# Attention with a learned bias, then a max-of-three layer: fewer identity products, other PSUM banks and another pace in the first steps

## The chip, the cores and the metric

The kernel runs on one NeuronCore of one Trainium2 chip. The metric is device time in microseconds (us): the median of three runs.

## What is computed

The first stage is attention for 4 batches, 8 heads, 576 positions and 64 features, with a bias that a small two-layer network makes of the distance of two positions. The second stage multiplies its output by three matrices, takes the largest of the three products and multiplies by a fourth.

```python
scores = scale * np.matmul(q, k.transpose(0, 1, 3, 2))
rel = (pos[:, None] - pos[None, :]).astype(np.float32)
x = (np.log1p(np.abs(rel)) / psi_i)[..., None]
bias = np.maximum(x @ w1 + b1, 0.0) @ w2
scores = scores + bias.transpose(2, 0, 1)[None, :, :, :]
attn = np.exp(scores - np.max(scores, axis=-1, keepdims=True))
attn = attn / (np.sum(attn, axis=-1, keepdims=True) + 1e-09)
x = (attn @ v)            # then laid out as 2304 tokens by 512
h = np.maximum(np.maximum(x @ w1, x @ w2), x @ w3)
return h @ w_out
```

## The kernel before

**Bias stage.** 36 groups of 16 rows: VectorE (DVE) and ScalarE (ACT) make the hidden layer, TensorE (PE) multiplies by `w2s` into `bp` tiles of two PSUM banks, DVE or ACT scale them into `bs`, and SyncE's queue (SP) writes them to DRAM as `bias_d`, from where the tiles `bias0` to `bias4` are read. Ahead of it stand four products `wps` of a tile of zeros.

**Attention stage.** Heads go in pairs; a unit is one pair of heads of one batch, and 16 units make 8 pairs of units. A pair of units has nine steps (`NS` = 9), so 72 steps are numbered n = 0 to 71, and a step's place in its pair is n % 9. Each step takes 128 query rows of two heads; one of the nine (`y == MIX`) takes the 64 rows left over of both units. What step n does, by function:

- `front(n)`: PE makes the scores `s` of both heads, two tiles of two PSUM banks each: 12 products, as the operands are split into a high part (`kh`, `qh`) and a low part (`kl`, `ql`). In the first `FILL` = 4 steps four products of the identity (L265), whose result is overwritten at once, stand ahead of them. In these four steps the score tiles rotate through four buffers, eight banks; afterwards through two buffers, four banks, and the other four banks hold `l`, `t` and `pv`.
- up to three items are taken from the list `pvq` (L422 on): an item is one block of the product of attention and values (`pv`), five items make a group, and `pv` is a single bank. The first item of a group first calls `split_x`, which writes the DVE copies (`xb`) of the group before into the program.
- `shift(n, h)`: DVE adds the bias to the scores and finds the minimum `nm` (L290), for each of the two heads; `expo(n, h)`: ACT makes the exponentials (L304).
- `norm(n-2)`: GpSimd (POOL) multiplies by the reciprocal of the sums (L318). `flip(n-4)`: PE transposes (tiles `tp`, `lp`), and ACT (L431, L432) and DVE (L434) copy the result into `et`. Where a group of transposes is complete (`ends`), the second exponential of the step stands behind these copies instead of ahead of them.
- `prep`: the split of a later unit's operands. ACT makes the high parts `kh`, `qh` (L242), POOL subtracts for the low parts `kl`, `ql` (L245).
- the stream `w0`: conversion of the weights of the second stage from 64-bit words, one instruction per step at most: one on ACT (L546) and four on DVE (L548, L550, L553, L556) for each half block, with sums and differences on POOL behind some of them. From step 7 on, each step but those with n % 9 == 8 carries one.

Each engine runs its instructions in the order in which these calls write them; nothing reorders them, so an instruction that waits holds up all behind it on its engine.

**Second stage.** Products `c` and `p` in three operand terms each, at L605 to L607 and L975 to L977, with DVE and ACT combining them.

## Time and profile before

| | |
|---|---|
| median of three runs | 554.94 us (554.85 to 555.05) |
| the profiled execution | 554.69 us |
| its span, first to last instruction | 552.9 us |
| busy in the span | PE 530.2, DVE 438.9, ACT 363.3, POOL 293.2 us |
| chain that ended last | PE 78%, DVE 10%, ACT 5%, issue 4% |

In a row of the windows view stand the stretch in us, its length, the busy time and in brackets the instructions of PE, PE's weight loads (PEld), DVE, ACT and POOL, PE's granted clock, the DMA engines' busy share and GB/s. In a timeline row stand start, length, engine, line, operation, output and inputs, shapes, count, and in square brackets the idle time before it and what ended it.

The span is cut here by the first `shift` of a pair of units: the bias stage ends at 51.76 us, the attention steps run to about 270 us, and the second stage starts at 282.4 us. A busy PE is modelled and says little by itself; the waits at its side, and which instruction stands ahead of the one that waited, say more.

### The profile page before, as it was taken

How to read it: one execution, taken by the hardware profiler on the slowest of the kernel's cores; microseconds unless marked ns; L12 is line 12 of the kernel's file. 1: busy time of each engine (PE TensorE's matmuls, PEld its weight loads, DVE VectorE, ACT ScalarE, POOL GpSimd, SP SyncE). 2: the span in 40 equal slices, each digit the busy share in tenths (PEclk: the TensorE clock that was granted, in tenths of full speed). 3: DMA queues.
4: the chain of work that ended last, by engine and by line, in shares of the span. 5: the costliest groups of instructions: out<-in, count | busy, mean ns of one | idle time of the engine just before them, and what ended most of it. 6: DMA issues, size and time to landing. Idle time of an engine off the chain costs nothing.

```text
span 552.9 us, 13740 instructions
## 1 busy us (share of the span) xinstructions
PE 530.2 (96%) x5231; PEld 438.3 (79%) x5231; DVE 438.9 (79%) x913; ACT 363.3 (66%) x814; POOL 293.2 (53%) x296
## 2 busy tenths in 40 slices
PE   8999888999999999999899999999999999999997
PEld 4456655666666666666589999999999999999997
DVE  7997668999988998887588888866887346798883
ACT  6997787898999989898766633434334335355552
POOL 0847475598988989766700328366386433600000
PEclk9999889999999999999999999999999999999999
DMA  5895971954594219311100424542256330467562
GB/s 142 226 342 163 337 241 23 304 196 144 146 340 125 58 25 297 90 24 40 43 2 2 152 77 135 190 153 78 76 207 212 116 127 16 140 205 210 178 186 76
DMA packets 74033, 80.75 MB, mean 146 GB/s; under 512 B 23216, under 2 KB 54576, under 8 KB 73968
## 3 DMA queue, kind: packets, MB, share of 16 engines
q1 hardware_dynamic: 73824, 79.58, 45.8%
q8 instruction: 41, 0.67, 0.5%
q10 hardware_dynamic: 144, 0.29, 0.2%
q14 instruction: 24, 0.20, 0.1%
HBM read 50.61 MB, written 28.99 MB: 144 GB/s over the span
## 4 chain that ended last, share of the span: by engine, by line
PE 78%; DVE 10%; ACT 5%; issue 4%; DMA 1%; POOL 1%; SPq 0%; DVEq 0%; ACTq 0%
PE pv L386 11%; PE p L607 10%; PE p L606 10%; PE p L605 10%; PE s L280 7%; PE tp L345 4%; PE p_o L977 4%; PE p_o L975 4%; PE p_o L976 4%; DVE hid L114 4%; PE bp L135 3%; ACT e L304 3%; DVE sn L290 2%; PE lp L345 2%; PE c L605 2%
## 5 line engine op out<-in xcount | busy, mean ns | idle before, releaser
L318 POOL TENSOR_SCALAR e<-e,rc 128x576 f32<-128x576 f32 x144 | 112.7, 801 | 36.0 <-DVE rc L314 28.6
L304 ACT ACTIVATE e<-sn,nm 128x576 f32<-128x576 f32 x144 | 111.5, 776 | 23.4 <-DVE nm L290 22.9
L290 DVE CUSTOM_DVE_ANT_0 sn<-s,bias 128x576 f32<-128x576 f32 x144 | 103.1, 753 | 19.6 <-PE s L280 11.6
L386 PE MATMUL pv<-et,vt 128*64 128x320 f32 (+1 forms) x496 | 75.2, 424 | 3.9 <-DVE xb L405 1.8
L497 POOL TENSOR_TENSOR wl<-wr,wh 128x256 fp32r<-128x256 f32 x25 | 23.6, 969 | 74.7 <-ACT wh L693 74.7
L434 DVE COPY et<-tp 128x512 f32<-128x512 f32 x72 | 49.0, 680 | 17.2 <-PE tp L345 13.9
L345 PE MATMUL tp<-ident,e 64*128 64x64 f32 x1152 | 55.3, 227 | 0.0
L280 PE MATMUL s<-kh,qh 64*128 64x288 f32 x256 | 51.2, 340 | 3.8 <-DVE nm L290 3.7
L386 PEld LDWEIGHTS pv<-et,vt 128*64 128x64 f32 x496 | 31.7, 138 | 29.1 <-issue 6.2
L245 POOL TENSOR_TENSOR kl<-kr,kh 128x576 fp32r<-128x576 f32 x16 | 39.4, 2462 | 24.1 <-ACT kh L242 23.0
L345 PEld LDWEIGHTS lp<-ident,e 64*128 64x128 f32 x144 | 19.8, 138 | 35.3 <-issue 23.4
L431 ACT COPY et<-tp 128x512 f32<-128x512 f32 x72 | 41.3, 574 | 8.6 <-PE lp L345 6.1
L345 PEld LDWEIGHTS tp<-ident,e 64*128 64x128 f32 x1152 | 45.4, 140 | 0.1
L135 PE MATMUL bp<-hid,w2s 128*32 128x79 f32 (+51 forms) x640 | 41.4, 401 | 3.3 <-DVE hid L114 2.1
L280 PE MATMUL s<-kl,qh 64*128 64x288 f32 x256 | 44.3, 299 | 0.0
L280 PE MATMUL s<-kh,ql 64*128 64x288 f32 x256 | 43.2, 296 | 0.9 <-POOL ql L245 0.9
L114 DVE TENSOR_SCALAR hid<-sm,bp 128x528 f32<-128x528 f32 (+17 forms) x108 | 41.4, 458 | 0.0
L345 PE MATMUL lp<-ident,e 64*128 64x64 f32 x144 | 35.3, 245 | 5.2 <-ACT et L432 2.7
L135 PEld LDWEIGHTS bp<-hid,w2s 128*32 128x32 f32 x640 | 20.6, 113 | 24.6 <-issue 15.5
L497 POOL TENSOR_TENSOR wl<-ws,wh 128x256 fp32r<-128x256 f32 x28 | 29.5, 1076 | 14.3 <-ACT wh L695 14.3
L280 PEld LDWEIGHTS s<-kh,qh 64*128 64x128 f32 x256 | 30.7, 191 | 7.1 <-DVE nm L290 6.2
L652 ACT COPY u<-p 128x384 f32<-128x384 f32 x24 | 11.5, 480 | 37.0 <-PE p L607 37.0
(229 smaller groups left out, 1622.0 us busy)
## 6 DMA issues: line engine op xcount, KB each, us to landing
bias_d<-bs SPq DMA_DIRECT2D x36, 295.5 KB, 5.5
bias<-bias_d SPq DMA_DIRECT2D x16, 576.0 KB, 6.0
w<-in_moe_w_dram SPq DMA_DIRECT2D x36, 256.0 KB, 3.3
h_d<-ht SPq DMA_DIRECT2D x18, 384.0 KB, 3.4
hin<-h_d SPq DMA_DIRECT2D x16, 384.0 KB, 4.6
qr<-in_qd_dram SPq DMA_DIRECT2D x16, 288.0 KB, 4.6
kr<-in_kd_dram SPq DMA_DIRECT2D x16, 288.0 KB, 5.3
vt<-in_v_dram SPq DMA_DIRECT2D x32, 128.0 KB, 2.9
```

The lines of the kernel that those rows point to most:

```text
L114: nc.vector.tensor_scalar(out=h[:, 0:n], in0=wl[:, 0:n], scalar1=k["bp"][:, m:m + 1], scalar2=0.0, op0=ALU.add, op1=ALU.max)
L135: nc.tensor.matmul(bp[32 * c:32 * c + 32, o:o + w], lhsT=w2s, rhs=src, start=True, stop=True)
L280: nc.tensor.matmul(ss[h][:, x, 0:HALF], lhsT=u[q][p, 128 * t:128 * t + 128], rhs=u[k][p, cols], start=(j == 0), stop=(j == 2))
L290: nc.vector.tensor_tensor_reduce(out=sn.rearrange("p (a b) -> p a b", a=2), in0=st["s"][h][:, :, 0:HALF], in1=bt.rearrange("p (a b) -> p a ...
L304: nc.scalar.activation(st["e"][:, S * h:S * h + S], sn, ACTF.Exp, scale=-1.0, bias=nm, accum_out=self.sm[:, x:x + 1])
L318: nc.gpsimd.tensor_scalar(out=e, in0=e, scalar1=self.rc[:, x:x + 1], scalar2=1.0, op0=ALU.mult, op1=ALU.mult)
L345: return nc.tensor.transpose(to, e2[p, k0:k0 + 128], ident[p, p])
L386: nc.tensor.matmul(pv[p], lhsT=w, rhs=x, start=(c == 0), stop=(c == NTQ))
L497: eng.tensor_tensor(out=out, in0=f(a), in1=f(b), op=op)
L605: nc.tensor.matmul(o, lhsT=hi[:, c], rhs=h[:, j], start=first and j == 0, stop=False, **on)
L606: nc.tensor.matmul(o, lhsT=hi[:, c], rhs=l[:, j], start=False, stop=False, **on)
L607: nc.tensor.matmul(o, lhsT=lo[:, c], rhs=h[:, j], start=False, stop=last and j == 1, **on)
```

## The change

- One of the four products of zeros ahead of the bias stage goes. As the bias products rotate through the same banks, each of them moves by one place.
- Identity products: none in step 0, two instead of four in steps 1, 2 and 3.
- The score tiles of the first four steps are two tags of two buffers, `s0` for even steps and `s1` for odd ones. As built, the two tiles of steps 0 and 2 lay in the banks from 0 and from 6 on, those of steps 1 and 3 in those from 4 and from 2 on; now steps 0 and 2 have 0 and 2, steps 1 and 3 have 4 and 6. From step 4 on the tiles lie at 0 and 2, before and now. The second tile of step 4 therefore waited for step 3, and now waits for step 2; the first transposes, at 4 to 6, now wait for step 3.
- In the first 18 steps at most three items of `pvq` are taken and none after the last of a group. Before, up to three were taken in the first 16 steps without regard to groups, and by the table after that.
- For the third unit (steps 6 and 7) DVE, not ACT, makes `kh` and `qh`.
- `ends` also holds for n % 9 == 7.
- The stream `w0` rests at n % 9 of 4, 5 and 8 instead of 8 alone.

On PE, the end of the bias stage (`bp31`) and step 0 (tiles `s0_0_0`, `s0_0_1`), before:

```order
L135 MATMUL bp31_881<-hid126_859,w2s_98 32x80
L135 MATMUL bp31_881<-hid127_857,w2s_98 32x80
L265 MATMUL s0_0_0_905<-ident_63 128x128 x4
L280 MATMUL s0_0_0_905<-kh0_244,qh0_320 128x288
L280 MATMUL s0_0_1_906<-kh0_244,qh0_320 128x288
L280 MATMUL s0_0_0_905<-kl0_245,qh0_320 128x288
```

and now:

```order
L134 MATMUL bp31_879<-hid126_857,w2s_96 32x80
L134 MATMUL bp31_879<-hid127_855,w2s_96 32x80
L279 MATMUL s0_0_0_903<-kh0_242,qh0_318 128x288
L279 MATMUL s0_0_1_904<-kh0_242,qh0_318 128x288
L279 MATMUL s0_0_0_903<-kl0_243,qh0_318 128x288
L279 MATMUL s0_0_1_904<-kl0_243,qh0_318 128x288
```

The four identity products between the last bias product and the first scores are gone.

On DVE, steps 10 and 11, where a group of products ends (`sn10`, `sn11` are the shifts, `wa3` the conversion), before:

```order
L314 RECIPROCAL rc8_1447<-sm8_1318 128x4
L434 COPY et1_1_1269<-tp0_6_1_1453 128x8x64
L548 TENSOR_SCALAR wa3_0_1411<-wa3_0_1411 128x512
L405 COPY xb11_0_1219<-pv0_1_1431 128x128
L405 COPY xb11_1_1223<-pv0_1_1431 128x128
L405 COPY xb11_1_1223<-pv0_1_1431 128x64
L290 ISA sn11_0_1506,nm11_0_1507<-s1_2_0_1482,bias2_76 128x576
L290 ISA nm11_0_1507 128x1
```

and now:

```order
L313 RECIPROCAL rc8_1435<-sm8_1306 128x4
L434 COPY et1_1_1255<-tp0_6_1_1441 128x8x64
L548 TENSOR_SCALAR wa3_0_1399<-wa3_0_1399 128x512
L289 ISA sn11_0_1488,nm11_0_1489<-s1_2_0_1470,bias2_76 128x576
L289 ISA nm11_0_1489 128x1
L289 ISA sn11_1_1493,nm11_1_1494<-s1_2_1_1471,bias2_76 128x576
L289 ISA nm11_1_1494 128x1
L405 COPY xb11_0_1207<-pv0_1_1419 128x128
L405 COPY xb11_1_1211<-pv0_1_1419 128x128
L405 COPY xb11_1_1211<-pv0_1_1419 128x64
```

The three copies of `pv0_1` stood between the conversion of step 10 and the shift of step 11, and now stand behind that shift. The same holds for the copies of `pv1_1` at steps 12 and 13.

On DVE, steps 22 and 23 (n % 9 of 4 and 5), before:

```order
L290 ISA nm22_1_2228 128x1
L556 SCALAR_TENSOR_TENSOR wr1_2231<-w642_0_1646,signm_64,wa2_0_1972 128x512
L314 RECIPROCAL rc20_2237<-sm20_2097 128x4
L434 COPY et4_0_2241<-tp2_0_1_2244 128x8x64
L290 ISA sn23_0_2294,nm23_0_2295<-s2_5_0_2276,bias0_74 128x576
L290 ISA nm23_0_2295 128x1
L290 ISA sn23_1_2299,nm23_1_2300<-s2_5_1_2277,bias0_74 128x576
L290 ISA nm23_1_2300 128x1
L405 COPY xb12_1_1222<-pv3_0_2214 128x192
L405 COPY xb12_2_1226<-pv3_0_2214 128x64
L434 COPY et4_0_2241<-tp2_1_1_2308 128x8x64
L548 TENSOR_SCALAR wa2_1_2236<-wa2_1_2236 128x512
```

and now:

```order
L289 ISA nm22_1_2211 128x1
L313 RECIPROCAL rc20_2214<-sm20_2074 128x4
L434 COPY et4_0_2218<-tp2_0_1_2221 128x8x64
L289 ISA sn23_0_2270,nm23_0_2271<-s2_5_0_2252,bias0_74 128x576
L289 ISA nm23_0_2271 128x1
L289 ISA sn23_1_2275,nm23_1_2276<-s2_5_1_2253,bias0_74 128x576
L289 ISA nm23_1_2276 128x1
L405 COPY xb12_1_1210<-pv3_0_2197 128x192
L405 COPY xb12_2_1214<-pv3_0_2197 128x64
L434 COPY et4_0_2218<-tp2_1_1_2284 128x8x64
```

The conversion instructions L556 and L548 no longer stand in these steps. The last conversion on DVE was in step 48, and now is in step 63.

```diff
--- before.py
+++ after.py
@@ -45,11 +45,10 @@
 
     const = ctx.enter_context(tc.tile_pool(name="const", bufs=1))
     psums = []
-    s_bufs = [4]
     dram = ctx.enter_context(tc.tile_pool(name="dram", bufs=1, space=DRAM))
 
-    def ps_s(name):
-        return psums[-1].tile([128, 2, 512], F32, tag="s", bufs=s_bufs[-1], name=name)
+    def ps_s(name, tag="s"):
+        return psums[-1].tile([128, 2, 512], F32, tag=tag, bufs=2, name=name)
 
     def bank(name):
         return psums[-1].tile([128, 512], F32, tag="p", bufs=8, name=name)
@@ -259,9 +258,9 @@
         def front(self, n):
             pair, y = fronts[n]
             which, t = step_of(pair, y)
-            ss = [ps_s(f"s{pair}_{y}_{h}") for h in range(2)]
+            ss = [ps_s(f"s{pair}_{y}_{h}", f"s{n % 2}" if n < FILL else "s") for h in range(2)]
             terms = (("qh", "kh"), ("qh", "kl"), ("ql", "kh"))
-            for _ in range(4 if n < FILL else 0):
+            for _ in range(2 if 0 < n < FILL else 0):
                 nc.tensor.matmul(ss[0][:, 0, 384:512], lhsT=ident, rhs=ident, start=True, stop=True)
             for x in range(2):
                 cols = slice(HALF * x, HALF * x + HALF)
@@ -395,6 +394,7 @@
                                     self.done.append((pv[:, o + lo - col:o + hi - col],
                                                       raws[x][slot][:, hp % 2, lo - TW * x:hi - TW * x]))
                             o += w
+                        return True
                 return run
 
             self.wait = True
@@ -418,12 +418,12 @@
                     self.load_v(2 * pair + (y == 7))
                 self.front(n)
             back = 0 <= f < NSTEP
-            for _ in range((3, 2, 3, 2, 3, 2, 2, 2, 1)[n % NS] if n >= 16 else 3):
-                if self.pvq:
-                    self.pvq.pop(0)()
+            for _ in range((3, 2, 3, 2, 3, 2, 2, 2, 1)[n % NS] if n >= 2 * NS else 3):
+                if self.pvq and self.pvq.pop(0)() and n < 2 * NS:
+                    break
             done = [(un, g) for at, un, g in ((MIX if fronts[f][0] else 3, 0, 1), (1, 0, 0), (6, 1, 1), (8, 1, 0))
                     if back and fronts[f][1] == at]
-            ends = bool(done)
+            ends = bool(done) or n % NS == 7
             rest = []
 
             def empty():
@@ -466,7 +466,7 @@
                 k = n - (NS * pair + (3 if pair else 6))
                 if 0 <= k < 2 and 2 * pair + 2 < len(units):
                     if k == 0:
-                        self.splits = self.prep(2 * pair + 2)
+                        self.splits = self.prep(2 * pair + 2, None if pair else nc.vector)
                     next(self.splits)
                 if pair and y <= 1:
                     if y == 0:
@@ -1057,7 +1057,7 @@
         bp = tc.alloc_tile_pool(name="bias_p", bufs=1)
         warm = bp.tile([128, 256], F32, name="warm")
         nc.vector.memset(warm, 0.0)
-        for k in range(4):
+        for k in range(3):
             wps = psums[-1].tile([128, 1024], F32, tag="bp", bufs=4, name=f"wps{k}")
             nc.tensor.matmul(wps[:, 0:256], lhsT=warm[:, 0:128], rhs=warm, start=True, stop=True)
         for g, _ in enumerate(bias_stage(bp)):
@@ -1085,7 +1085,6 @@
             if n == FILL:
                 psums.pop().release()
                 psums.append(tc.alloc_tile_pool(name="psum", bufs=1, space=PSUM, reuse_waits="tile"))
-                s_bufs.append(2)
             at.step(n)
             for f in kept[:3] if n > 1 else ():
                 kept.pop(0)()
@@ -1195,7 +1194,7 @@
         ex, lx = Stream(early_x()), Stream(late_x())
         while n < NSTEP + LAG:
             more = []
-            if n >= NS - 2 and n % NS != NS - 1:
+            if n >= NS - 2 and n % NS not in (4, 5, 8):
                 more += [w0]
             if n >= 36 and n % NS in (2, 6, 7):
                 more.insert(0, ex)
```

## Rows read from the trace of the kernel before

**Rows 1.** Windows, pairs 0, 1, 3, 6, second stage (columns below).

```profile
51.76:76.49 24.73, 20.37 (x250) 15.87 (x252) 16.94 (x46) 20.01 (x53) 12.48 (x16) 0.93 0.84 280
76.49:107.78 31.29, 28.02 (x356) 18.74 (x356) 24.81 (x65) 24.10 (x63) 20.30 (x23) 0.95 0.54 154
...
135.09:161.90 26.81, 26.11 (x357) 17.74 (x358) 24.45 (x64) 25.14 (x67) 25.49 (x30) 1.00 0.66 196
...
217.90:243.66 25.76, 25.40 (x354) 17.30 (x350) 21.09 (x59) 23.74 (x65) 19.48 (x24) 1.00 0.34 101
...
282.40:552.00 269.60, 266.83 (x1721) 265.92 (x1719) 202.47 (x303) 121.16 (x221) 91.93 (x89) 1.00 0.40 130
```

**Rows 2.** Timeline of steps 0 to 4: start, length, instruction, idle before and its releaser.

```profile
49.57 1.16 PE L265 MATMUL s<-ident 128*128 128x128 f32 x8
...
51.76 0.76 DVE L290 CUSTOM_DVE_ANT_0 sn<-s,bias 128x576 f32<-128x576 f32 x1 [2.35 <-DMA bias_d<-bs]
...
59.68 0.39 PE L280 MATMUL s<-kh,qh 64*128 64x288 f32 x1 [1.25 <-DVE nm L290]
...
60.75 0.76 DVE L290 CUSTOM_DVE_ANT_0 sn<-s,bias 128x576 f32<-128x576 f32 x1 [1.13 <-PE s L280]
```

**Rows 3.** Timeline, operands of the third unit: a cast on ACT, and PE's wait.

```profile
73.43 0.69 ACT L242 CAST qh<-qr 128x576 fp32r<-128x576 f32 x1
...
75.67 0.40 PE L280 MATMUL s<-kh,ql 64*128 64x288 f32 x2 [0.86 <-POOL ql L245]
```

**Rows 4.** Timeline at the group ends of steps 11 and 13.

```profile
83.50 0.31 PE L280 MATMUL s<-kh,ql 64*128 64x288 f32 x2
...
85.11 0.62 DVE L405 COPY xb<-pv 128x128 f32<-128x128 f32 x3 [1.15 <-PE pv L386]
...
85.65 0.75 DVE L290 CUSTOM_DVE_ANT_0 sn<-s,bias 128x576 f32<-128x576 f32 x1
...
90.70 1.20 PE L273 MATMUL s<-kr,qr 64*64 64x288 f32 x16
...
93.20 0.75 DVE L290 CUSTOM_DVE_ANT_0 sn<-s,bias 128x576 f32<-128x576 f32 x1
```

**Rows 5.** Windows view, steps 22 and 23, 40 and 41, 58 and 59; columns as rows 1.

```profile
120.41:127.35 6.94, 6.94 (x94) 4.78 (x92) 6.94 (x16) 6.74 (x19) 6.94 (x8) 1.00 0.76 206
174.52:181.99 7.47, 7.01 (x96) 4.75 (x94) 6.94 (x14) 7.02 (x19) 6.04 (x7) 1.00 0.50 132
230.41:235.93 5.52, 5.52 (x82) 4.00 (x80) 4.67 (x14) 5.49 (x16) 4.39 (x5) 1.00 0.47 137
```

**Rows 6.** Timeline: conversions on DVE in steps 19 and 41, and POOL beside the second.

```profile
113.61 0.51 DVE L548 TENSOR_SCALAR wa<-wa 128x512 f32<-128x512 f32 x1
...
180.37 1.42 POOL L245 TENSOR_TENSOR ql<-qr,qh 128x576 fp32r<-128x576 f32 x1
...
180.54 1.53 DVE L550 TENSOR_SCALAR wa<-wa 128x512 uint32<-128x512 uint32 x1
```

**Rows 7.** Timeline of SP and ACT around the first transfer of weights.

```profile
71.02 1.97 SPq L539 DMA_DIRECT2D w<-in_moe_w_dram  x2
...
80.33 0.67 ACT L546 ACTIVATE wa<-w 128x512 f32<-128x512 f32 x1
```

**Rows 8.** View of the tile w from 70 to 79 us, four transfers.

```profile
DMA to landing us min/median/max: 3.6/4.7/5.5
```

**Rows 9.** Windows view of one stretch; columns as rows 1.

```profile
64.10:67.51 3.41, 3.41 (x36) 2.75 (x36) 2.05 (x6) 2.59 (x7) 1.20 (x2) 0.50 0.95 340
```

**Rows 10.** Pieces of the chain that ended last: start, length, instructions.

```profile
65.11 1.55 PE s L280 x12
66.65 1.88 PE pv L386 x12
...
69.24 0.88 PE s L280 x11
...
96.06 1.45 PE pv L386 x12
```

## The prediction

> **What bounds the kernel now.** I read the windows view first, cut by pairs of units, then the timeline of the first two pairs, then the chain that ended last, and then what else uses the time that the chain shows. In the second stage PE is busy in 266.8 of 269.6 us [rows 1]. The change does not touch that stage, so it moves as a block: what the attention steps gain is gained at the end. In the attention steps a pair of units costs 24.7 us (pair 0, in which most of the first six steps have no product of attention and values), 31.3 us (pair 1), 26.8 us (pair 3) and 25.8 us (pair 6) [rows 1]. Pair 6 carries no conversion, and PE is busy in 25.4 of its 25.8 us: this is what a pair costs when PE sets the pace. Pair 1 lies 5.5 us above it and its PE is idle for 3.3 us, so the first pairs wait for something that is no PE work. What a step is worth is read at its shift, because DVE's shift waits for the scores of its step, PE's next scores wait until the shift has freed their banks, and ACT's exponentials follow the shift.
>
> **Steps 0 to 4: identity products and banks.** Step 0's identity products run from 49.57 for 1.16 us, and the first shift comes at 51.76 [rows 2]. Without them the first scores follow the last bias product directly; their operands are there, since they start right behind the identity products now. That is 1.1 us. The product of zeros at the start cost nothing: PE waits for the hidden layer behind it in any case. In steps 1 to 3 two of four products go, 0.58 us of PE each by the same row. These steps are paced by PE until ACT's two exponentials become the bound; I take 1.4 us of the 1.7. In step 4 the second head's scores wait 1.25 us for step 3's shift, because the two tiles share banks [rows 2]; the new places put the wait on step 2, whose shift is over by then. The first transposes inherit the wait on step 3, but they need normalized exponentials from POOL and stand behind the scores in any case. That is 1.2 us more, 3.7 in all at the shift of step 4, now at 60.75 [rows 2]. What is late next is ACT: it then runs exponentials without a gap, and its copies of the transposes release PE's next transposes. I keep 3.5 us; the bounds are 1.1 (only step 0) and 4.0 (every wait gone).
>
> **Operands of the third unit.** ACT's cast of 0.69 us ends at 74.12, POOL's subtraction follows, and PE waits 0.86 us for `ql` [rows 3]. On DVE the cast is made while ACT works on its exponentials, so POOL starts when it is free. I take 0.6 us. The trace has no such cast on DVE. The nearest rows are fast conversions of 512 columns, 0.51 us alone and 1.53 us beside a POOL subtraction that runs at the same time [rows 6]. The latter costs 1.0 us per cast more, and shifts stand behind both casts, so the bounds are a loss of 1.4 and a gain of 0.9. The row of 0.51 is the nearer one, as POOL's subtraction waits for the cast and so cannot run beside it; normalizations can.
>
> The Trainium skill speaks against this edit: by SBUF — State Buffer, section "Who interferes with whom", DVE copies and casts in a two-port mode and GpSimd hold the shared port for a whole instruction and the other one blocks. The row of 1.53 us agrees, as it ends only after POOL's 1.42 us are over.
>
> **Group ends.** At step 11 the scores are done at 83.81, but the shift starts at 85.65, since three copies of the group's product stand ahead of it on DVE and wait 1.15 us for PE [rows 4]. At step 13 the scores end at 91.90 and the shift starts at 93.20, for the same reason [rows 4]. With the stop at a group's end the copies stand behind the shift. That is 1.8 and 1.3 us, 3.1 in all. The products left out are made one step later, in steps that had fewer: by step 19 as many are done as before. I take 3.0; the bounds are 1.3 and 3.6.
>
> **Against it, the transfers.** SP's queue is full in these steps and does not move with them. The weights' first two transfers are issued from 71.02 on for 1.97 us and land 3.6 to 5.5 us after their issue [rows 7, 8], so the second lands between 76.6 and 78.5; ACT converts them at 80.33 [rows 7]. With 4.1 us gained by then ACT arrives at 76.2 and waits 0.4 to 2.3 us, with the exponentials of step 10 behind it. Part of that goes into ACT's slack: I take 0.8 us of loss, bounds 0 and 2.3.
>
> **Conversions.** Steps 22 and 23 take 6.94 us with DVE busy throughout, 40 and 41 take 7.47 us; steps 58 and 59, the same places without conversions, take 5.52 us [rows 5]. That is 1.4 and 1.9 us. They are dear there because POOL's subtractions run in these steps: the conversion at 180.54 takes 1.53 us where one at 113.61 took 0.51 [rows 6]. Steps 13 and 14 lose one instruction each too; I add 0.7 us, half of the smaller gain. Against this, eight conversions move to steps 52 to 63. Pair 3, which has seven on DVE, costs 1.05 us more than pair 6 [rows 1]; pair 6 now gets six of them and pair 7 two, and I charge 1.1 us. Net 2.9 us, bounds 1.0 and 4.0. The conversions take their transfers on SP and their sums on POOL along (the last sums from steps 48 to 51 to steps 64 to 68). I cost that at nothing, because a bias tile is fetched four steps ahead of its use, which hides a transfer queued in front of it; without that cover it is one landing, up to 5.5 us [rows 8]. The order of the exponentials at n % 9 == 7 I cost at nothing: the copies release PE's transposes sooner and one exponential comes later, of which the sums are wanted only a step later; without that cover it is one copy's time per pair, so up to 1 us either way.
>
> **Sum.** 3.5 + 0.6 + 3.0 - 0.8 + 2.9 = 9.2 us of the profiled execution's 554.69, which is 545.5; the median of the runs lies 0.25 higher, within the rounding. Of the 554.69 the span is 552.9, and the 1.8 around it stay.
>
> **Rivals.** *The transfers set the pace.* For: SP's queue is full, and from step 9 on ACT waits for weights. Then of the 4.1 us gained in pair 0 only 80.33 - 78.5 = 1.8 are left, 2.3 lost in place of the 0.8, and the group ends behind it run into the transfers of the values, which are queued next; I estimate another 0.5. That is 7.2 us gained, 547.5. Against: the steps after 10 need little that is not landed.
>
> *The port.* For: both casts and three of the fast conversions moved to pair 6 meet POOL as at 180.54. Each costs 1.0 us more, and two of the conversions fall beside subtractions: 4 us, so 5.2 gained, 549.5. The rule of the page named above is this case; by its order of issue, whoever comes first holds the port.
>
> *The clock, some.* The granted clock was 0.50 from 64.10 to 67.51, half of 2.4 GHz [rows 9], after steps in which PE had waited. In such a stretch twelve score products take 1.55 us where eleven take 0.88, and twelve products with values 1.88 where 1.45 is normal [rows 10]: 1.1 us for a step. Pairs 0 and 1 have two stretches of it. Fewer identity products leave PE less to do in steps 1 to 3, and three further stretches (or a later rise at the start, where a product of zeros is gone) would cost about 3.5 us: 549.0. Against: the steps come closer together, so PE waits less.
>
> The Trainium skill, TensorE: Matmul & The Clock Gate, Part 1, has the low clock as the default that activity lifts, which is what the identity products stand for.
>
> *Slower.* The same clock, but held: with half the identity products gone PE falls to 1.2 GHz in step 1 and stays there, since ACT paces these steps and PE keeps waiting. At 1.1 us a step the gain of 9.2 us is used up after eight or nine steps; through twelve steps it costs 13.2 us and the kernel ends 4 us slower, 558.7. Against: once products with values come (step 6), steps are full of PE work, and before, the clock came back after one stretch.
>
> *The change does what it says.* The order of instructions shows each part in place, so no case is kept for that.
>
> **How the numbers follow.** The sum 0.60; transfers 0.15; port 0.12; clock in part 0.10; slower 0.03. The upper ends of all terms together, with 1 us for the exponentials' order, are 13.5 us, which is 541.2. Port and clock in part lie at 549.0 and 549.5, and the lower ends of two or three terms together reach the same place; I end the range at 541.0 and 550.5. Left out are the slower case, a part of the clock's and the port's cases, and gains over 13.7 us. About 0.2% (1.1 us) is what a measurement of this kernel can tell from no change. All cases but the last are faster than that: faster 0.95, the same 0.02 (a clock case between the two), slower 0.03.
>
> **What the profile after would show.** Right: the first shift near 50.7; step 4's shift near 57; no wait of the second head's scores there; the shifts of steps 11 and 13 directly behind their scores; pair 1 near 27 us instead of 31.3; steps 22, 23, 40 and 41 near 2.8 us each; pair 6 about 1 us longer than 25.8; the second stage unchanged at 269.6 us. Wrong: ACT waiting at the first weights' conversion for more than 2 us (transfers); casts on DVE of over 1 us (port); more than two stretches at half clock in the first two pairs (clock). If pair 1 stays above 29 us, the copies at the group ends only hid another wait.

## The result and the profile after

| | before | after |
|---|---|---|
| median of four runs each, side by side | 554.89 us (553.62 to 555.05) | 545.48 us (545.0 to 548.54) |
| the same, a second time (15 and 6 runs) | 554.94 us (551.58 to 558.5) | 545.48 us (544.88 to 546.08) |
| profiled execution, its span | 554.69 us, 552.9 | 545.0 us, 543.2 |

The ratio is 0.9847 (95% interval 0.9808 to 0.9886), the second time 0.9831 (0.9801 to 0.9861). The prediction said 545.5 us. That the sum came out is not the same as that its terms did; several of them did not.

The windows view after, cut at the first shifts of pairs 0, 1 and 6, and the second stage; columns as in [rows 1]:

```profile
49.58:71.46 21.88, 18.86 (x234) 14.31 (x234) 17.54 (x49) 18.36 (x51) 13.68 (x17) 0.92 0.83 276
71.46:98.17 26.71, 26.23 (x356) 18.26 (x358) 24.02 (x63) 24.24 (x64) 20.72 (x23) 1.00 0.73 209
...
206.18:233.16 26.98, 26.69 (x354) 18.10 (x354) 24.49 (x65) 24.54 (x66) 19.12 (x23) 1.00 0.33 102
271.90:543.22 271.32, 267.05 (x1721) 265.94 (x1719) 202.25 (x303) 121.07 (x221) 91.79 (x89) 1.00 0.39 129
```

Pair 0 took 24.73 us and now 21.88, pair 1 31.29 and now 26.71, pair 6 25.76 and now 26.98 [rows 1]. From its first product to the end of the span the second stage took 270.5 us and now 271.3; the 269.6 us of the prediction end with the row of [rows 1] at 552.00, 0.9 us ahead of the span's end.

The timeline after, steps 0 and 4 and the casts of the third unit (start, length, instruction, idle before and its releaser):

```profile
48.48 0.40 PE L279 MATMUL s<-kh,qh 64*128 64x288 f32 x2
...
49.58 0.76 DVE L289 CUSTOM_DVE_ANT_0 sn<-s,bias 128x576 f32<-128x576 f32 x1 [1.27 <-DMA bias_d<-bs]
...
56.02 0.75 DVE L289 CUSTOM_DVE_ANT_0 sn<-s,bias 128x576 f32<-128x576 f32 x1
...
65.34 0.59 DVE L243 CAST kh<-kr 128x576 fp32r<-128x576 f32 x1
...
68.13 0.45 DVE L243 CAST qh<-qr 128x576 fp32r<-128x576 f32 x1
```

The first scores follow the last bias product, and the shift of step 4 stands behind step 3's with no wait, where there were 1.13 us [rows 2]. DVE's casts take 0.59 and 0.45 us.

DVE at steps 11 to 13, where a group of products ends, with the last score products of steps 11 and 13, answering [rows 4]:

```profile
77.04 0.29 PE L279 MATMUL s<-kh,ql 64*128 64x288 f32 x2
...
77.08 0.82 DVE L548 TENSOR_SCALAR wa<-wa 128x512 f32<-128x512 f32 x1
77.83 0.74 DVE L289 CUSTOM_DVE_ANT_0 sn<-s,bias 128x576 f32<-128x576 f32 x1
...
79.17 0.61 DVE L405 COPY xb<-pv 128x128 f32<-128x128 f32 x3
79.70 1.14 DVE L550 TENSOR_SCALAR wa<-wa 128x512 uint32<-128x512 uint32 x1
...
82.77 1.38 PE L272 MATMUL s<-kr,qr 64*64 64x288 f32 x16
...
84.26 0.74 DVE L289 CUSTOM_DVE_ANT_0 sn<-s,bias 128x576 f32<-128x576 f32 x1
```

The shift of step 11 starts ahead of the group's three copies now, and none stand ahead of step 13's, at 84.26. The conversion behind the copies took 1.14 us. The scores of step 11 are done at 77.33 and its shift starts 0.50 us later, as a conversion of 0.82 us stands ahead of it; those of step 13 are done at 84.15, 0.11 us before its shift.

ACT's first conversion of weights, answering [rows 7]:

```profile
75.61 0.70 ACT L546 ACTIVATE wa<-w 128x512 f32<-128x512 f32 x1 [0.22 <-DMA vl<-in_v_dram]
```

It waited 0.22 us. The profile names the transfer of a value here, but the conversion reads weights alone, and in the variant with the old conversions the same wait, 1.45 us there, is put down to weights; so which of the two it was stays open.

The windows of the one stretch at half clock, and of steps 22 and 23, 40 and 41, 58 and 59, answering [rows 9] and [rows 5]:

```profile
59.37:62.78 3.41, 3.16 (x32) 2.74 (x34) 1.55 (x4) 2.60 (x8) 1.18 (x2) 0.50 1.04 355
111.14:116.76 5.62, 5.62 (x82) 4.18 (x82) 4.65 (x14) 5.59 (x16) 5.54 (x6) 1.00 0.76 218
164.40:170.03 5.63, 5.52 (x81) 4.04 (x80) 4.60 (x12) 5.60 (x17) 4.08 (x4) 1.00 0.43 130
219.23:225.23 6.00, 6.00 (x85) 4.35 (x87) 4.64 (x14) 5.96 (x16) 4.82 (x5) 1.00 0.45 129
```

At the first shift of a step, the kernel after was ahead by 2.18 us (step 0), 4.73 (step 4), 5.03 (step 9), 9.61 (step 18), 12.16 (step 45), 10.50 (step 63), and by 9.7 at the end.

### The profile page after: what moved, and what is told of

Its sections match the earlier page's. It is cut to its first block, busy times and chain, and to the rows that moved or that the text cites. A ratio compares the mean times of both kernels' runs of the same rounds, so it can differ in the third digit from the quotient of the medians.

```text
span 543.2 us, 13700 instructions
## 1 busy us (share of the span) xinstructions
PE 526.1 (97%) x5209; PEld 435.5 (80%) x5209; DVE 441.3 (81%) x915; ACT 362.0 (67%) x812; POOL 295.8 (54%) x296
## 4 chain that ended last, share of the span: by engine, by line
PE 58%; DVE 2%; DMA 1%; ACT 1%; issue 1%; DVEq 0%; ACTq 0%
PE p L607 11%; PE p L605 11%; PE p L606 11%; PE pv L385 5%; PE p_o L977 3%; PE p_o L975 3%; PE p_o L976 3%; PE s L279 3%; PE tp L344 2%; PE c L605 2%; PE c L606 2%; PE c L607 2%; DMA hin<-h_d 1%; PE lp L344 1%; PE s L272 1%
## 5 line engine op out<-in xcount | busy, mean ns | idle before, releaser
L244 POOL TENSOR_TENSOR kl<-kr,kh 128x576 fp32r<-128x576 f32 x16 | 41.3, 2583 | 19.3 <-ACT kh L241 18.8
```

## The experiments

Each kernel is the one after with one edit, but for the kernel after once more and, at the end, the kernel before. Times stand against 545.5 us. Executions of one kernel differ by 1 to 2 us and at times more, for reasons that the last section gives, so steps are compared in the traces as well.

### Four products of zeros

```diff
-        for k in range(3):
+        for k in range(4):
             wps = psums[-1].tile([128, 1024], F32, tag="bp", bufs=4, ...
```

> The changed kernel with the fourth product of zeros put back at the start; nothing else differs. In the trace of the changed kernel the first shift came at 49.58 us, 2.2 us before its old place of 51.76, where 1.1 was expected from step 0's identity products; the last bias product ended at 48.45 instead of 49.6, and TensorE's granted clock was full from 4.75 us on instead of 9.48. Theory A (the removed product moves the bias products' banks and the clock's rise, and is worth 1.1 us): the clock rises near 9.5 us, the first shift is near 50.7, the time near 546.6. Theory B (the product costs nothing; the early rise belongs to the one execution that was profiled): the first shift stays near 49.6 or moves without the product's doing, and the time stays at 545.5.

Measured: 546.71 us. PE's and DVE's timeline at step 0:

```profile
48.66 0.40 PE L279 MATMUL s<-kh,qh 64*128 64x288 f32 x1
49.60 0.40 PE L279 MATMUL s<-kh,qh 64*128 64x288 f32 x1 [0.54 <-ACT bs L157]
...
50.57 0.76 DVE L289 CUSTOM_DVE_ANT_0 sn<-s,bias 128x576 f32<-128x576 f32 x1 [2.07 <-DMA bias_d<-bs]
```

The clock was full from 4.82 us on here, as in the first profile of the kernel after, so the fourth product has no part in that, as theory B has it. Yet the first shift came at 50.57, and neither theory had the reason: the scores of the second head wait for ACT's last scaling (`bs`). The product shifts the bias tiles by one place, so that the last of them, `bp31`, lies in banks 2 and 3, where the new places put step 0's second tile. From the last bias products on, step 0 is 0.81 us later than without it. The removed product belongs to the new banks: beside them it is worth 0.8 us, while with the old places neither number shows this wait (four in the kernel before, three in the variant with the old banks).

### The old rule at the ends of groups

```diff
-            for _ in range((3, 2, ...)[n % NS] if n >= 2 * NS else 3):
-                if self.pvq and self.pvq.pop(0)() and n < 2 * NS:
-                    break
+            for _ in range((3, 2, ...)[n % NS] if n >= 16 else 3):
+                if self.pvq:
+                    self.pvq.pop(0)()
```

> The changed kernel with the old rule for the products of attention and values: up to three per step in the first 16 steps, then the table, without a stop at a group's end. Theory A (the copies of a group's product that stand ahead of the shifts of steps 11 and 13 cost 3.0 us): the shifts of steps 11 and 13 again come 1.8 and 1.3 us after their scores, steps 9 to 17 take about 30 us instead of 26.7, and the time is 548.5. Theory B (the products that the stop puts off are paid for in the steps after): steps 10 and 12 get longer but 11, 13 and 14 shorter, and the time is at most 546.5. The time from step 18 on should be as in the changed kernel under both.

Measured: 548.29 us, 2.8 more. DVE's timeline at steps 11 and 13:

```profile
78.49 0.62 DVE L405 COPY xb<-pv 128x128 f32<-128x128 f32 x3 [0.74 <-PE pv L385]
79.03 0.74 DVE L289 CUSTOM_DVE_ANT_0 sn<-s,bias 128x576 f32<-128x576 f32 x1
...
86.04 0.62 DVE L405 COPY xb<-pv 128x128 f32<-128x128 f32 x3 [0.21 <-PE pv L385]
86.57 0.74 DVE L289 CUSTOM_DVE_ANT_0 sn<-s,bias 128x576 f32<-128x576 f32 x1
```

The copies stand ahead of both shifts again. Against the first profile of the kernel after it was 0.14 us ahead at step 10, 2.31 behind at step 13 and 2.99 at step 18. Theory A stands: 2.5 to 3.1 us, all of it by step 18. Steps 9 to 17 took 29.84 us here and 26.71 in the first profile of the kernel after, but ACT waited 1.17 us for its first conversion here, and 0.22 there; the variant of the last but one experiment, which waited 1.19 us, took 27.32.

### The old conversions

```diff
-            if n >= NS - 2 and n % NS not in (4, 5, 8):
+            if n >= NS - 2 and n % NS != NS - 1:
```

> The changed kernel with the weights' conversions in every step from 7 on but those with n % 9 = 8, as before, so that the last on DVE falls in step 48 and not 63. Theory A (conversions in the places 4 and 5 meet POOL's subtractions and are dear, net 2.9 us): steps 22 and 23 take 6.9 us instead of 5.6, steps 40 and 41 7.5 instead of 5.6, pair 6 (steps 54 to 62) 25.8 instead of 27.0, and the time is 548.4. Theory B (what the later steps and the second stage pay takes nearly all of it back: between step 18 and the end the changed kernel gained 0.1 us only): the same steps change as under A, but steps 45 to 62 get shorter by 2 us or more and the second stage by 0.8, and the time is 545.5 to 546.3.

Measured: 547.57 us, 2.1 more. Windows of steps 22 and 23, 40 and 41, and of pairs 5 and 6; then pair 5 of the kernel after:

```profile
112.17:119.09 6.92, 6.92 (x94) 4.77 (x91) 6.92 (x16) 6.72 (x19) 6.92 (x8) 1.00 0.78 220
166.60:174.06 7.46, 7.01 (x96) 4.75 (x94) 6.94 (x15) 7.02 (x19) 6.03 (x7) 1.00 0.50 130
182.15:209.94 27.79, 26.97 (x357) 18.47 (x358) 24.71 (x64) 24.56 (x66) 25.69 (x28) 1.00 0.45 127
209.94:235.72 25.78, 25.65 (x354) 17.34 (x350) 21.09 (x59) 23.83 (x65) 19.46 (x24) 1.00 0.32 97
```

```profile
177.84:206.18 28.34, 27.45 (x357) 18.61 (x358) 26.90 (x64) 25.89 (x69) 26.22 (x29) 1.00 0.48 134
```

The two places cost 1.30 and 1.83 us more than after (5.62 and 5.63 above): these readings held. What pairs 5 and 6 pay for the later conversions is 55.32 less 53.57, which is 1.75 us, where I had charged 1.1. Steps 18 to 62 took 136.17 us here, 1.3 more than in the second profile of the kernel after (134.90, shown below). Another 1.1 us lies in steps 9 to 17 (27.84 against 26.71), but the variant without identity products, with the new conversions, took 27.86 there, and in both ACT waited some 1.5 us for its first conversion; so this part isn't shown to be the conversions'. Steps 13 and 14, for which 0.7 us was added, took 5.64 us here and 5.69 after: nothing. Theory A has the sign and place right, at somewhat under a half to three quarters of its size.

### The old banks

```diff
-            ss = [ps_s(f"s{pair}_{y}_{h}", f"s{n % 2}" if n < FILL else "s") for h in range(2)]
+            ss = [ps_s(f"s{pair}_{y}_{h}") for h in range(2)]
```

and `s` with four buffers in the first four steps, then two.

> The changed kernel with the old score tiles of the first four steps: one tag with four buffers, so that the second tile of step 4 lies in banks of step 3. Theory A (the wait of step 4's second scores for step 3's shift is worth 1.2 us): these scores wait about 1.2 us again, the shift of step 4 comes 1.2 later behind step 3's, and the time is 546.7. Theory B (ACT paces these steps: the shift of step 4 comes later, but the exponentials of steps 3 to 5 end where they ended, or the first transposes lose their own wait for step 3): the first shifts from step 6 on are less than 0.4 us later, time 545.5 to 545.9.

Measured: 546.38 us. PE at step 4:

```profile
56.97 0.40 PE L280 MATMUL s<-kh,qh 64*128 64x288 f32 x1 [1.25 <-DVE nm L290]
```

The wait of 1.25 us [rows 2] is back to the hundredth, and the shift of step 4 comes 1.22 us later behind step 3's. That much of theory A holds. Its time lies 0.9 above, but its runs spread over 5.9 us, so how much reaches the end is not settled by the median. By the traces most of it does: from the first shift to that of step 9 it took 22.91 us here and 21.88 in the first profile of the kernel after, to that of step 63 184.39 and 183.58, each with one stretch of 3.4 us at half clock.

### The kernel after once more

> The changed kernel once more, nothing edited, as the base on this chip for the others of this group and as a second profile. In the first profile the clock was full from 4.75 us on, the first shift came at 49.58, and a stretch at half clock (59.37 to 62.78) cost 1.15 us at step 6 against two variants without one. Theory A (clock and landing times at the start differ from execution to execution): with a rise near 10 us the first shift is at 50.4 to 50.7 whatever the number of zero products, the shifts of steps 1 to 5 keep their distances to it, and step 6 lies at 62.4 where no half-clock stretch falls on step 5. Theory B (the early start belongs to this kernel): first shift at 49.6 again.

Measured: 545.48 us. The clock rose at 10.28 us, the first shift came at 50.40 us: theory A. The distances of steps 1 to 4 to the first shift are those of the first profile to 0.01 us. That of step 5 isn't: its shift came 0.71 us later, as it waited 1.10 us for a bias tile to land. The second profile of the kernel before has the same wait of 1.10 us, so it doesn't come from the change.

### No identity products

```diff
-            for _ in range(2 if 0 < n < FILL else 0):
+            for _ in range(0):
```

> The changed kernel without the two identity products of steps 1, 2 and 3: none at all are left. Theory A (ACT's two exponentials of 0.78 us each set these steps of 1.63 to 1.74 us, and PE is no longer late): steps 1 to 3 get at most 0.2 us shorter each, step 4 comes at most 0.5 us sooner, time 545.0 to 545.5. Theory B (PE still sets them): another 0.44 us a step, 1.3 in all, time 544.2. Theory C (the clock needs them): TensorE's granted clock falls to 0.5 in more stretches between steps 1 and 8 than the one of the changed kernel, each of them 1.1 us, time 546.6 or more.

Measured: 545.29 us. Steps 0 and 1 got 0.27 and 0.38 us shorter and step 2 not at all, since ACT's exponentials set the pace there; the clock stayed full throughout. At step 4 that is 0.64 us, more than theory A allowed (0.5) and half of what B did (1.3). Little of it is left: ACT then waits 1.58 us for its first conversion, and steps 9 to 17 take 27.86 us. The time is theory A's, and C is out: the products that are left hardly cost anything in the end, and in this profile the clock did not need them.

### Rest at the places 4 and 5 only

```diff
-            if n >= NS - 2 and n % NS not in (4, 5, 8):
+            if n >= NS - 2 and n % NS not in (4, 5):
```

> The changed kernel with conversions at n % 9 = 8 too, so that only the places 4 and 5 rest (seven a pair instead of six, the last on DVE some nine steps sooner). In the trace of the changed kernel, steps at place 8 take 2.46 to 2.55 us, all of it PE. Theory A (only places beside POOL's subtractions are dear; a conversion at place 8 fits beside PE): steps at place 8 get at most 0.3 us longer, steps 54 to 62 fall from 27.0 towards 25.8, time 0.5 to 1 us below the changed kernel. Theory B (any DVE instruction more in a pair delays its shifts): each of the pairs from 18 on with seven is 0.4 us or more longer, and the time is the same or up to 0.5 us above.

Measured: 551.17 us, 5.7 more; neither theory. ACT's first conversion:

```profile
79.10 0.66 ACT L546 ACTIVATE wa<-w 128x512 f32<-128x512 f32 x1 [6.99 <-DMA w<-in_moe_w_dram]
```

With no rest in step 8 it comes one step sooner and waits 6.99 us for the first weights, with the exponentials behind it. Steps 9 and 10 take 8.18 and 5.96 us, and in that wait the clock fell to half, from 77.46 to 84.28. This is the rival of the transfers, at a price above the one I gave it. What keeps it away after is the rest in step 8 (before, too).

### Rest at 2, 4 and 5

```diff
-            if n >= NS - 2 and n % NS not in (4, 5, 8):
+            if n >= NS - 2 and n % NS not in (2, 4, 5):
```

> The changed kernel with conversions at place 8 instead of place 2 (rests at 2, 4 and 5; the number per pair is unchanged). In the traces, steps at place 2 of pairs 2, 4 and 6 take 3.72, 3.53 and 3.73 us with a conversion there or one step before, and 3.16, 2.92 and 3.22 in the variant with the old conversions. Theory A (place 2 is dear, since the six conversions bunch at 0 to 3; place 8 is free): steps 18 to 62 are 0.4 us a pair shorter, 2 us in all, time 543.5. Theory B (the cost only moves to place 8, or into the next shift at place 0): the pairs keep their lengths within 0.2 us, time 545.5.

Measured: 549.61 us, 4.1 more. The first conversion is early here as well and waits 2.42 us; steps 9 and 10 take 3.60 and 5.87 us. Steps 18 to 62 take 134.20 us, against 134.90 in the second profile of the kernel after: theory A in sign, 0.7 us instead of 2. Place 8 is not free: its steps in pairs 2 to 5 took 3.12 to 5.06 us with the conversion, and 2.46 to 2.55 without.

### The third unit on ACT

```diff
-                        self.splits = self.prep(2 * pair + 2, None if pair else nc.vector)
+                        self.splits = self.prep(2 * pair + 2)
```

> The changed kernel with the third unit's two casts on ACT again. In the changed kernel DVE makes them in 0.59 and 0.45 us, and steps 6 to 8 together take 8.95 us. Theory A (ACT's cast made POOL's subtraction and PE's scores late, 0.6 us): PE waits for ql again before the shift of step 9, steps 6 to 8 take about 9.5 us, time 546.1. Theory B (ACT has the time, or DVE's casts delay shifts by as much): steps 6 to 8 within 0.2 us of 8.95, time 545.5.

Measured: 548.5 us, 3.0 more. PE's wait, and the windows row of the half-clock stretch behind it:

```profile
71.23 0.40 PE L279 MATMUL s<-kh,ql 64*128 64x288 f32 x2 [0.89 <-POOL ql L244]
```

```profile
73.38:76.80 3.42, 3.24 (x17) 2.22 (x19) 2.25 (x8) 2.57 (x8) 1.43 (x2) 0.50 1.01 310
```

The wait for `ql` is back (0.89 us, 0.86 before [rows 3]), and steps 6 to 8 take 9.38 us instead of 8.95: directly 0.4 us. But the clock fell behind it, and four of the six runs had a mean granted clock of 0.987 or 0.988; these took 548.4 to 551.2 us, the other two 546.3 and 547.6. All runs of the next two kernels, on the same chip, had 0.993 or more. So against the median after the edit is worth 0.8 us where the mean clock was 1.000 and 2.2 in the profiled run (0.997, with the stretch above), and more in the other four. One run in ten of the kernel after took 548.54 us too, so how much of the 3.0 is the edit's is not settled.

### The old order at place 7

```diff
-            ends = bool(done) or n % NS == 7
+            ends = bool(done)
```

> The changed kernel with the second exponential ahead of the copies again at n % 9 = 7. Theory A (nothing: PE sets the pace of these steps, and neither the copies nor the exponential are late): steps at the places 7 and 8 keep their lengths within 0.1 us, time 545.5. Theory B (the copies release PE's transposes sooner, and that is worth something in each of eight pairs): 0.1 to 0.3 us a pair, time 546.3 or more. Theory C (the later exponential costs): 544.7 or less.

Measured: 544.19 us, 1.3 less: theory C, with five of six runs below the lowest of the kernel after. Windows of steps 18 to 62 here, and in the second profile of the kernel after:

```profile
99.26:232.81 133.55, 130.97 (x1770) 89.31 (x1766) 123.97 (x316) 124.37 (x330) 112.85 (x124) 1.00 0.52 158
```

```profile
99.37:234.27 134.90, 132.81 (x1770) 90.06 (x1768) 124.84 (x316) 124.73 (x330) 112.45 (x124) 1.00 0.52 157
```

That is 1.35 us. In steps 9 to 17 this profile lost as much (27.98 us against 26.53), though hardly by the order: the variant without identity products, with the new order, took 27.86 there, and ACT's first conversion waited in both, here for

```profile
77.12 0.69 ACT L546 ACTIVATE wa<-w 128x512 f32<-128x512 f32 x1 [1.91 <-DMA vt<-in_v_dram]
```

DVE in step 52, a step at place 7, here and after:

```profile
202.66 0.43 DVE L548 TENSOR_SCALAR wa<-wa 128x512 f32<-128x512 f32 x1
203.01 0.16 DVE L313 RECIPROCAL rc<-sm 128x4 f32<-128x4 f32 x1
203.10 0.65 DVE L434 COPY et<-tp 128x512 f32<-128x512 f32 x1
203.80 0.76 DVE L289 CUSTOM_DVE_ANT_0 sn<-s,bias 128x576 f32<-128x576 f32 x1
```

```profile
201.93 0.17 DVE L313 RECIPROCAL rc<-sm 128x4 f32<-128x4 f32 x1
202.12 0.69 DVE L434 COPY et<-tp 128x512 f32<-128x512 f32 x1
202.73 0.98 DVE L548 TENSOR_SCALAR wa<-wa 128x512 f32<-128x512 f32 x1
203.63 0.74 DVE L289 CUSTOM_DVE_ANT_0 sn<-s,bias 128x576 f32<-128x576 f32 x1
```

`ends` moves more than the exponential: the free conversion of the step, too, goes behind the copies. After, it took 0.98 us right ahead of the next shift; here 0.43 us ahead of them, while PE still made the transposes. Step 52 takes 2.50 us instead of 3.06.

### Rest at 4 and 5, and in step 8

```diff
-            if n >= NS - 2 and n % NS not in (4, 5, 8):
+            if n >= NS - 2 and n % NS not in (4, 5) and n != NS - 1:
```

> The variant that rests at the places 4 and 5 only, with one more rest, in step 8; from step 17 on place 8 carries a conversion. In that variant ACT's first conversion came one step sooner, and waited 6.99 us for the first weights to land; steps 9 and 10 took 8.18 and 5.95 us instead of 2.58 and 3.78. Theory A (the whole loss is that one wait; a conversion at place 8 costs little later): steps 9 and 10 are back at 2.6 and 3.8 us, steps 18 to 62 take 133.4 to 134 us instead of 134.9, time 544.5 to 545.2, below the changed kernel. Theory B (place 8 is dear in every pair): steps 18 to 62 take 135.5 us or more and the time is 546 or more.

Measured: 546.06 us. Steps 9 and 10 are back at 2.58 and 3.76 us, so nearly the whole loss of the variant without that rest comes from the one wait, as theory A says. Steps 18 to 62, though:

```profile
98.36:233.52 135.16, 132.77 (x1770) 90.24 (x1766) 124.24 (x316) 124.38 (x330) 115.80 (x128) 1.00 0.52 156
```

A conversion at place 8 saves nothing either: 135.16 against 134.90 us.

### The kernel before once more

> The kernel before, unedited, for a second profile. In its first profile the second stage took 270.50 us from its first product, in six profiles of the changed kernel and its variants 270.87 to 272.35, with a wait of 0.44 to 0.50 us for one sum on DVE that the kernel before did not show. Theory A (the landing of one transfer of hin differs from execution to execution): the second stage takes 270.9 or more here too, or 270.5 with an earlier landing. Theory B (the change moves transfers into the second stage, or their place): 270.5 again, without that wait. Of the clock: two or three stretches at half clock before 90 us, as the mean clock of 0.991 to 0.994 of most runs of it says, against one in the changed kernel (0.997).

Measured: 556.48 us, in one profiled execution. Its half-clock stretches; then DVE in the second stage, at the sum that waits for the transfer `hin`, here and after:

```profile
61.80:68.63 6.83, 6.75 (x48) 5.21 (x50) 4.63 (x12) 5.15 (x14) 2.92 (x4) 0.50 0.97 321
78.87:82.28 3.41, 3.33 (x17) 2.23 (x19) 2.15 (x8) 3.38 (x10) 1.41 (x2) 0.50 0.70 242
```

```profile
501.60 0.56 DVE L497 TENSOR_TENSOR C<-hin,hin 128x384 f32<-128x384 f32 x1 [0.28 <-DMA hin<-h_d]
```

```profile
491.76 0.56 DVE L497 TENSOR_TENSOR C<-hin,hin 128x384 f32<-128x384 f32 x1 [1.94 <-DMA hin<-h_d]
```

The second stage took 271.3 us here, as long as after, with products that ran 4% slower for a part of it (twelve in 1.41 us, where 1.36 is usual); so a second stage of 270.5 is not a property of this kernel. The wait for `hin` is: 0.28 and 1.12 us in its two profiles, 1.94 and 1.71 in those of the kernel after, and with it a later sum for which PE waits 0.43 to 0.50 us in all twelve profiles of the kernel after and its variants, and in neither of before.

## Why the prediction was right, term by term

All numbers are us gained; in the last column stands how much the median rose when the part was undone.

| term | predicted | measured in the traces | undone, median |
|---|---|---|---|
| steps 0 to 4 | 3.5 | 1.1 + 1.3 + 1.2 = 3.6 | 0.9 (banks alone) |
| third unit's casts | 0.6 | 0.4 directly, and the clock | 3.0 |
| group ends | 3.0 | 2.5 to 3.1 | 2.8 |
| transfers | -0.8 | -0.2 | |
| conversions | 2.9 | 1.3 to 2.3 | 2.1 |
| order at place 7 | 0 | -1.4 | -1.3 |
| second stage | 0 | -0.4 to -0.8 | |

**Right.** The steps with identity products got 0.44 us shorter each, step 4's wait of 1.25 us is gone, and the shifts of steps 11 and 13 come 0.50 and 0.11 us behind their scores instead of 1.84 and 1.30. Pair 1 took 26.7 us (announced near 27), and steps 22, 23, 40 and 41 took 2.8 us each. Of the 2.18 us at step 0, 1.09 is no gain of the change: in that execution the bias stage itself ended as much sooner, and in eight of the ten other profiles with three products of zeros the first shift lay at 50.3 to 50.7 us, where it was announced. The stretch at half clock from 59.37 to 62.78 gave it back: step 5 took 3.99 us with it, 2.83 or 2.84 in five variants without it.

**The conversions** were over-valued at their far end. The two pairs of steps gave what their rows said; the steps that took the conversions over were charged by the difference of pairs 3 and 6, 1.1 us, and cost 1.75, as pair 5 got longer too. The 0.7 us that was added for steps 13 and 14 isn't found in them. In the argument on the port, three conversions meet POOL and only two are charged; no run bears on that count.

**The third unit** was under-valued. The direct part is the wait of the row; that a stretch at half clock may follow such a wait was kept as a rival for the change's loss only, and not as part of its gain.

**The order at place 7** is the step that failed. Its sign was left open within 1 us; the text weighed copies against an exponential and missed the conversion that the same condition moves.

**The rivals.** The transfers lost 0.2 us in the first profile and nothing in the second, thanks to the rest in step 8 and to the stretch at half clock, which let ACT come later: of the profiles with that rest, the three with such a stretch ahead of step 9 show a wait of ACT for its first conversion of 0.22 us at most, the seven without one 0.70 to 1.91 us. In four of these seven the group ends and the conversions are those of the kernel after, and steps 9 to 17 took 27.15 to 27.98 us instead of 26.71 and 26.53. So 0.8 was a fair price, and that it was hardly paid is luck. Nor did the queue stand still: the first weights were issued at 69.95 us, where it had been 71.02, and at 70.16 to 71.67 in those four. The port fell: casts of 0.59 and 0.45 us. The clock went the other way: 3.4 us at half clock in both profiles of the kernel after, 6.8 and 10.2 in those of the kernel before, and none where no identity product was left; the slower case falls with that. Pair 6, announced about 1 us longer, is 1.22 longer.

The measured terms add up to 5.6 to 7.2 us, with 0.6 for the second stage. Some 1.7 to 2.9 more came from the clock (last section), which makes 7.3 to 10.1 for the 9.4 measured. So the sum came out because a gain that was not in it paid for losses that were not in it: that it did so to 0.1 us is luck. The best kernel of these is the one after with the old order at place 7, 544.19 us, a ratio to before of 0.9816 (0.9784 to 0.9848). The interval overlaps that of the kernel after; what speaks for it is the 1.35 us in steps 18 to 62, and that at equal mean clock its median lies lower too, by 1.6 us at 0.996 or 0.997 (three runs against seven) and by 1.0 at 1.000 (two against two).

## What to carry to other kernels

Read an edit by everything that its condition moves: a flag that put one exponential behind the copies also moved a conversion to the spot right ahead of a shift, and cost 1.4 us. Where buffers change places, look who used the new place last: a product of zeros was worth 0.8 us because it decided where the last bias tile lay. And before an idle slot is filled, see what it hides: one more conversion in step 8 cost 5.7 us, as the slot covered a transfer. And what is gained ahead of a transfer can be given back where it is waited for: here a profile had either the stretch at half clock or a wait for the first weights of up to 1.9 us.

## What was not expected of the hardware

**The clock differs between executions of one kernel**, and most of the spread of the kernel before follows it. TensorE first had its full clock (2.4 GHz) at 4.75 to 12.6 us in the fourteen profiles of this study, and a rise near 4.8 ended the bias stage some 0.7 us sooner. The Trainium skill, TensorE: Matmul & The Clock Gate, Part 1, says that the gate runs free of the kernel's start, so that the moment of its change differs from run to run; these profiles agree. Of 37 runs of the kernel before, five with a mean granted clock of 1.000 took 551.3 to 552.1 us, six with 0.996 or 0.997 553.1 to 554.3, 17 with 0.993 or 0.994 554.6 to 556.2, and the nine others, with 0.990 or 0.991, 555.0 to 558.5. Seven of ten runs of the kernel after had 0.996 or 0.997 and took 545.0 to 546.1. At that clock the medians lie 7.7 us apart, at 1.000 (five runs and two) 6.5; I estimate from this that 1.7 to 2.9 of the 9.4 us are stretches at half clock (1.2 GHz) that most runs of the kernel after no longer have.

**Which engine came first** decided the price of a conversion. In step 11 of the kernel after it began 0.57 us behind a subtraction on POOL and took 1.14 us; in the variant with the old order at place 7 it began 0.39 us ahead of the same subtraction and took 0.41. The subtraction after, then both in that variant:

```profile
79.13 1.44 POOL L244 TENSOR_TENSOR ql<-qr,qh 128x576 fp32r<-128x576 f32 x1 [0.61 <-ACT qh L241]
```

```profile
80.22 0.41 DVE L550 TENSOR_SCALAR wa<-wa 128x512 uint32<-128x512 uint32 x1
...
80.61 1.41 POOL L244 TENSOR_TENSOR ql<-qr,qh 128x576 fp32r<-128x576 f32 x1 [2.47 <-ACT qh L241]
```

The Trainium skill, SBUF — State Buffer, section "Who interferes with whom", has it that order of issue decides which of the two blocks. These rows agree.

Open stays why the transfer `hin` lands later after the change (6.8 and 6.6 us from issue at the longest in this stretch, 5.3 and 4.8 before), though SP issues it between the same transfers, and why products ran 4% slower for a part of the second stage in some executions of both kernels.
